# Batch 0's squares: summed over the pairs of heads by GpSimd ahead of TensorE

## The chip, the cores and the metric

The kernel runs on one core of one Trainium2 chip. The metric is the device time of one execution in microseconds (us), lower is better. The kernel before takes 975.91 us, the median of three runs (975.13 to 976.47).

## The reference, cut to what matters

Attention with keys and values pooled over 8 tokens (8 batches, 8 heads, 576 tokens, head size 64) feeds a gated MLP on 4608 tokens of width 512 with 1536 hidden units. Between the two stands an RMS norm: each token's 512 values x are divided by the root of the mean of their squares.

```python
rms = np.sqrt(np.mean(x * x, axis=-1, keepdims=True) + 1e-06)
xn = x / rms * rms_g
g = xn @ w_gate
val = xn @ w_val
return (silu * val @ w_out).astype(np.float32)
```

The 512 values of a token are 4 pairs of heads of 128 values. Attention's result lies with these 128 values on the partitions and the tokens along the free axis, one tile per pair of heads. The sum of squares of a token therefore runs over 128 partitions and over four tiles.

## The kernel before, in words

Work is done in 8 batches of attention and in blocks of 512 tokens of the MLP, interleaved. The order of everything is one long string, ORDER, of short step names; an underscore marks steps of the opening stage (attention of batches 0 and 1, the unpacking of the weights, the first MLP block). Each engine (TensorE, VectorE, ScalarE, GpSimd) and the queue of SyncE, which issues all DMAs, carries out its own instructions strictly in the order of the string. Waits between engines are put in by the framework: an instruction waits for what it reads, and a tile that takes over a place in memory waits until everything that the program does with the previous tile of that place is done. A step's name ends in hexadecimal-like digits: its numbers; a digit behind ":" is the PSUM bank, one behind "/" the buffer that it takes.

The steps that matter here, each with its line or helper:

- `_A` (s_av, L560) multiplies probabilities and values into PSUM tile psx, half the tokens at a time; for example `_A030` and `_A031` for pair 3 of batch 0.
- `_Z` (s_xsq, L590, ScalarE) squares psx into columns 2S to 3S of the tile own(p) of its pair p. There are eight: four pairs, two halves.
- `_P` (s_tokens, L652, TensorE) multiplies 128-token pieces of those squares by a column of ones, which sums over the partitions: five pieces, so five products per pair. They are float32 products, and the profile has two rows for each. Pair p writes column t * 4 + p of the PSUM tile psr.
- `_p` (s_total, L657, VectorE) adds the four pairs' columns, `_r0` (s_root, L664, ScalarE) takes the root, `_s0` (s_unroot, L667, VectorE) the reciprocal, `_B00` (s_spread, L676, TensorE) spreads it over the partitions, `_n` (L1029, ScalarE) copies it out of PSUM, and `_u0` (first_gate, L1033, VectorE) is the first to use it: it multiplies the first gate's psg, which `_m000` to `_m003` (first_mm, L1049, TensorE) produced, by it.
- `_l` loads a packed piece of the weights (L307, SyncE), `_a` reads it on ScalarE (L318), `_b`, `_c`, `_d` go on with it on VectorE (L322, L326, L330), `_h` rounds it on ScalarE (L344), `_w` or `_W` takes the rest (L292, VectorE or GpSimd). `_l6` to `_h6` is piece 6.
- `_N` (s_norm, L468) normalises probabilities of batch 1 on GpSimd; `_T` (L536) transposes them on TensorE.
- `_J` (s_join) adds two pairs' squares on GpSimd. Before the change only batches 1 and up use it; it goes through cut, which splits the 576 columns into two adds of 288.

Two places in memory are shared. own(0), the tile with pair 0's squares, lies in the slot w1_10. Piece 6 is the whole of the first weight matrix's block f = 3, and its raw words go to the slot NF - 1 - f % 2 = 10, the same one:

```python
s["own"] = space1(NF - 2 - 2 * p, [P, 3 * S + SP + P], F32, f"own{p}")
raw[f] = space1((2, 3)[f] if f < 2 else NF - 1 - f % 2, [P, 2 * NC * P, 2], U32, f"wx{f}")
```

In ORDER `_P00` stands before `_l6`, and `_P01 _P02 _P03` behind it. `_a6` is ScalarE's next step behind `_Z31`; then come `_h` of piece d (13), `_x31`, `_r0`. PSUM bank 2 is psr's, and the next to take it is `_T101:2`, ahead of `_B00` on TensorE.

Of the kernel before, what the change touches and what calls it, by code (L numbers as in the profile page):

```python
# [27 lines left out]
TOK = P  # L28
OFFS = (0, 128, 256, 384, 448)
# [33 lines left out]
_m011 _m001 _m013 _D100 _a9/0 _m003 _n _W4 _m100:5 Wt0/1 _l8 _Y031 _c6 _d6 _W7 _v11 _a8 _T102 _u0 _G0 _h6 _A100:1/1
_S11:27 _b9 _C102 _c9 _d9 _M110 _h9 _m102 _E110 _b8 _m110 _m112 _M111 _F0 _w9 _m101 _W6 _c8 _i0/1 _L0 Wf00 _d8 _lb/0
_R110 _m111 _K12/1 _A101:4 _ab/1 _X101 _bb _B01:6 _h8 _H01 _cb _m103 _u1 wf01 _db Wf02 _E111 _w8 _G1 _m113 _F1 wh03/0
Wl03 _la _X100 _hb _Wb _lf/0 Wf03 ws03 _e2:0 _o0:7564 _aa _g2:3 _i1/1 _ba _ca _L1 wh02/1 _o1 wl02 _af/0 _u2 _G2 _R111
_bf _cf _F2 _N110 _Q10 wd0 _i2/1 _T110:2/1 _D110 _df _hf _Wf _da _j2 _ha _g3:1 _lc _q12 _e3:0 wh01/0 _V11/0 _u3 _G3
_wa ws02 _o2 _N111 _F3 _ac _bc _cc _dc _k13 _i3/0 _lh/0 _ah/1 _hc _g4 _T112:1 _bh _D112 _j3 _T111:3 _le _D111 _e4:0
_ch _u4 _dh _hh wl01 ws01 Wt1/0 wh04/0 _ae Wl04 _Wc Wf10 _S12:32 _lg _Wh Wf11 Wf12 wf13 _be _M120 _M121 ws04 _G4 _F4
wh11/1 wl11 _ce _de _A110:1 _v20/1 _V20/1 _Y110 ws11 _o3 _A111:1 wh13/0 wd1 _i4/0 Wt2/1 _E120 _g5:0 wh14/1 _R120 Wl14  # L70
ws14 Wf20 _li Wl13 _L4 ws13 _ag _o4 _bg _e6 _he _We Wf21 _u5 _cg _E121 _R121 _dg wf22 _N121 wh12/1 Wl12 _e5:2 ws12 _G5
_Y111 _T121:1/1 Wf23 _F5 _i5/0 wh23/0 _v12 _j5 _N120 _D121 Wl23 wh21/1 Wl21 _q13 _K13/1 _T122 _ai _bi _ll/0 _hg ws23
ws21 _Wg _g6 _u6 _V12/0 _D122 _lk _k20 _v13 _o5 _G6 wh22/1 _F6 _i6/1 _ci _S13:10 _M130 _T120:3 _di wh24/0 Wl24 _D120
_j6 wl22 _M131 _g7 _u7 _hi ws22 _e7 _ak _o6 _K20/1 _bk _ck _G7 _F7 ws24 _E130 _dk _A121:3 _al/1 _bl _cl _ln/1 _an/0
_bn _cn _dl _i7/1 _R130 _dn _E131 _R131 _N131 _A120:2 _Y120 _hn _Wn _j7 _Y121 _g8:1 _u8 _V13/0 _G8 _wi _N130 wd4 _e8:0
_F8 _hl _wl _lj/0 _aj/0 _bj _cj _lm/1 _am/1 _bm _dj _T131:1/1 _o7 _D131 _hk _T130 _D130 _q20 sc20:21 wd2 _Q11/0 _cm
_T132 _D132 _dm _Wk _hj _A130:3 _Y130 Wt3/1 Wf30 _A131 _Y131 Wf31 lv21/0 mx201/1 sb201 _hm _Wj _wm _J11 mx200/1 lk21
pv21/0 _e9 sb200 wh33/0 Wl33 ex201 _lo/0 _i8/1 _L8 _g9:1 _u9 _ga:0 wh31/1 _o8 Wl31 ex200 _Q12/1 Wf32 Wf33 _J12 _Q13/0
ws33 _G9 _F9 ws31 _J13 _i9/0 wh34/0 pk21/1 Wl34 ws34 sm201/0 _ao/1 _bo _co _do _ho wh32/0 _L9 _P10:2 _ea _o9 _Wo _ua
sm200/0 nm200 _Ga _lp/0 _r1 Wl32 zd2 ws32 _Fa _ia/0 lq21 _ap/1 _gb:3 Nm201 tr20/1 _bp _La _s1 _B11:1 wd5 _cp _dp _hp  # L80
_ub _Gb _H11 wt4/0 _B10 _H10 _wp _eb:2 dm20 _Fb _oa sc21:10 wf40 wh41/0 Wl41 _t0 ws41 _t1 _ib/1 _jb wf41 wh43/1 _ob
lk22 Wl43 _t2 ws43 _t3 dp20/0 me10:2 Zt00/1 mg10:3 ev03/0 Wf42 Zt01 Zf00 Zf01 zh03/1 mx210/0 st03 sb210 Zl03 pk22/1
mx211/1 ev00/0 zs03 Zf02 Wf43 sb211 ex210 sm210/1 lq22 kt1 zh02/1 Zl02 ex211 sm211/1 st00 Nm210 zs02 wh42/0 Wl42 Nm211
av200:4/1 xc200 ws42 ev02/1 st02 me12:1 sc22:47 gt10 vl10 wh44/0 Wl44 hi10/0 lk23 ev01/1 mx221/1 ws44 st01 tr21/0
mx220/0 sb220 sb221 Lo10 mg11:6 Zf03 gt11 me11:0 dm21 vl11 zh04/0 zh01/1 mo10:4657 hi11/1 Zl04 zs04 mg12:0 Lo11 Zl01
Wt5/1 Wf50 mo11 wf51 wh53/0 Wf52 Wl53 zs01 pk23/0 gt12 vl12 av201:3 dp21/1 av210 ex220 xc210 av211:2 sm220/0 xd20 Wf53
xd21 lv23/0 wh54/1 Wl54 ws53 lq23 zd3 Nm220 pv23/0 ex221 sm221/1 Nm221 ws54 mg13:1 xc201 wh51/0 Wl51 tr22/0 xc211
hi12/1 sc23:03 mx231/0 mx230/1 sb230 ex230 sb231 lk30 pk30/1 wh52/1 Wl52 Lo12 dm22 ex231 lq30 me13:2 sm231/0 gt13
sm230/1 Nm230 vl13 Nm231 tr23/0 lv22/1 pv22/1 mo12 dp22/1 mg14:0 hi13/1 Lo13 ws51 me14 gt14 sc30:20 vl14 av221:1
mx301/1 xd22 sb301 dm23 sq20 sq21/1 Jn21 ws52 Wt6/0 av220:3 Wf60 Wf61 xc221 lk31 dp23/1 xc220 sq22/1 ex301 Jn22  # L90
mx300/0 pk31/0 mo13 hi14/1 lv30/1 sb300 Wf62 Lo14 wh61/0 Wl61 ws61 wh63/1 Wl63 ws63 wf63 mg15:0 gt15 sm301/0 nm301
lk32 ex300 me15 pv30/1 av231:2 xc231 wh64/0 sm300/0 Nm300 Wl64 av230:1 mo14 wh62/1 Wl62 lv31/1 ws64 xc230 vl15 tr30/0
hi15/0 Lo15 pk32/1 lq31 mg16:0 pv31/0 gt16 Zt10/1 ws62 Zf10 zh11/0 zl11 Zt11 Zf11 Zf12 me16:1 zh13/1 xd23 mo15 Zl13
dm30 vl16 sc31:20 mx310/0 zs11 sb310 zs13 mg17:1 hi16/1 Lo16 dp30/1 zh12/1 Zf13 zh14/0 mx311/0 mo16 sb311 zd4 gt17
Zl12 Zl14 Wt7/0 Wf70 zs14 Wf71 Wf72 wf73 sq23/1 Jn23 zs12 me17 ex310 av300:1/0 wh72/0 sm310/1 ex311 sm311/0 wh71/1
Wl71 xc300 lq32 zd1 vl17 hi17/1 Nm310 wl72 ws72 ws71 wh73/0 sh2/0 wh74/1 Nm311 tr31/1 sc32:02 mx320/0 sb320 av301:3
xd30 Lo17 dm31 ex320 xc301 Wl73 mx321/1 Wl74 Wt8/0 sb321 Wf80 mg18:1 ws73 gt18 Wf81 lk40 Wf82 ws74 wh81/0 mo17 Sl2
# [1112 lines left out]
```

## Time and profile before

| | before |
|---|---|
| median of 3 runs | 975.91 us |
| the profiled execution | 976.88 us |
| its span, first to last instruction | 975.1 us |
| TensorE matmuls busy | 947.5 us (97%) |
| VectorE busy | 704.2 us (72%) |
| ScalarE busy | 492.9 us (51%) |
| GpSimd busy | 490.4 us (50%) |
| mean granted TensorE clock | 0.982 of full speed |

The span is 1.8 us shorter than the execution's own time. An engine's busy time says how much it did, not what set the end; the chain of waits, followed back from the last instruction, says that. In the opening stage the share of each engine changes from microsecond to microsecond, so it is read from the order of time of single instructions. All times in the rows are microseconds from the start of the span.

### The profile page before, as it was taken

The numbers are of one execution on the slowest core, as the hardware profiler recorded it, in microseconds if no ns is written. First come the engines' busy times: TensorE is split into PE (matmuls) and PEld (weight loads), VectorE is DVE, ScalarE is ACT, GpSimd is POOL, SyncE is SP. The second block draws the span as 40 slices with busy tenths as digits, with TensorE's granted clock in tenths as the row PEclk, the third lists the DMA queues.
The fourth block names the chain that finished last, engine by engine and source line by source line (L and its number), as shares of the span: only waits on it lengthen the run. The fifth ranks groups of instructions, "written<-read, shape, count | busy, mean of one in ns | idle before, by whom it ended". The sixth has DMA issues, their size and how long they took to land.

```text
span 975.1 us, 14181 instructions
## 1 busy us (share of the span) xinstructions
PE 947.5 (97%) x4670; PEld 752.2 (77%) x4670; DVE 704.2 (72%) x1134; ACT 492.9 (51%) x929; POOL 490.4 (50%) x618
## 2 busy tenths in 40 slices
PE   7799999999999999999999999999999999999997
PEld 6577677777777877877877777877877778888885
DVE  6989898978787888778787877755565884433333
ACT  5876675645555647555455456242543642213332
POOL 3355637222322324433455788432296894445785
PEclk7789999999999999999999999999999999999999
DMA  9537774665766569878887776768686465767646
GB/s 300 183 137 273 225 247 157 215 204 178 240 204 204 171 182 267 251 231 274 253 248 255 202 253 195 243 184 263 217 257 212 155 219 173 229 189 232 205 141 204
DMA packets 142296, 211.41 MB, mean 217 GB/s; under 512 B 12240, under 2 KB 78288, under 8 KB 140944
## 3 DMA queue, kind: packets, MB, share of 16 engines
q1 hardware_dynamic: 142224, 210.52, 68.8%
q8 instruction: 37, 0.61, 0.3%
q14 instruction: 35, 0.29, 0.1%
HBM read 154.24 MB, written 56.23 MB: 216 GB/s over the span
## 4 chain that ended last, share of the span: by engine, by line
PE 76%; DMA 5%; DVE 5%; POOL 5%; ACT 3%; issue 2%; SPq 1%; DVEq 0%; ACTq 0%; POOLq 0%
PE pxy L895 30%; PE psg L1059 15%; PE pf L975 15%; PE po L1093 7%; PE psx L560 3%; PE pss L478 3%; POOL w L292 2%; DMA pt<-rows 1%; DMA ring<-vs 1%; POOL xp L292 1%; POOL hl L292 1%; DMA ring<-vB 1%; DVE wt L326 1%; PE psr L652 1%; DVE wt L330 1%
## 5 line engine op out<-in xcount | busy, mean ns | idle before, releaser
L895 PE MATMUL pxy<-xp,wp 128*128 128x512 f32 x1512 | 361.1, 391 | 1.5 <-ACT o L1104 0.7
L895 PEld LDWEIGHTS pxy<-xp,wp 128*128 128x128 f32 x1512 | 282.3, 188 | 65.3 <-issue 2.5
L975 PE MATMUL pf<-fp,ring 128*128 128x512 f32 x756 | 189.8, 393 | 3.1 <-DMA ring<-vB 1.6
L1059 PE MATMUL psg<-xh,w 128*128 128x512 f32 x544 | 171.2, 396 | 1.4 <-DVE prob L495 1.0
L975 PEld LDWEIGHTS pf<-fp,ring 128*128 128x128 f32 x756 | 139.6, 188 | 39.6 <-DMA ring<-vs 3.9
L1059 PEld LDWEIGHTS psg<-xh,w 128*128 128x128 f32 x544 | 101.2, 189 | 26.5 <-DVE prob L495 1.4
L1059 PE MATMUL psg<-xl,w 128*128 128x512 f32 x272 | 106.7, 392 | 0.0
L292 POOL TENSOR_TENSOR hl<-act,hh 128x256 fp32r<-128x256 f32 x58 | 49.8, 878 | 111.5 <-ACT hh L1075 102.6
L292 POOL TENSOR_TENSOR fp<-fs,fp 128x256 fp32r<-128x256 f32 x108 | 81.1, 778 | 41.7 <-ACT fp L948 37.9
L292 POOL TENSOR_TENSOR fp<-act,fp 128x256 fp32r<-128x256 f32 x72 | 55.1, 786 | 83.1 <-ACT fp L948 81.8
L1093 PE MATMUL po<-w,hh 128*128 128x512 f32 x288 | 72.9, 390 | 0.0
L292 POOL TENSOR_TENSOR w<-wt,w 128x256 fp32r<-128x256 f32 x50 | 48.7, 1000 | 45.7 <-ACT w L344 45.7
L1093 PEld LDWEIGHTS po<-w,hh 128*128 128x128 f32 x288 | 54.1, 188 | 11.6
L292 POOL TENSOR_TENSOR fp<-hb,fp 128x256 fp32r<-128x256 f32 x68 | 54.5, 828 | 13.9 <-ACT fp L948 13.9
L1059 PEld LDWEIGHTS psg<-xl,w 128*128 128x128 f32 x272 | 51.4, 189 | 11.1
L1154 ACT COPY hb<-pxy 128x512 f32<-128x512 f32 x36 | 21.0, 586 | 72.7 <-PE pxy L895 72.7
L1161 DVE TENSOR_TENSOR u<-u,pxy 128x512 f32<-128x512 f32 x36 | 24.7, 685 | 38.0 <-PE pxy L895 37.8
L948 ACT CAST fp<-act 128x512 fp32r<-128x512 f32 x36 | 22.2, 619 | 58.5 <-DVE act L1162 49.3
L948 ACT CAST fp<-fs 128x512 fp32r<-128x512 f32 x54 | 33.0, 618 | 34.3 <-POOL fs L292 16.7
L1155 DVE TENSOR_TENSOR u<-hb,pxy 128x512 f32<-128x512 f32 x36 | 24.6, 684 | 33.3 <-PE pxy L895 19.7
L292 POOL TENSOR_TENSOR fs<-act,hb 128x256 f32<-128x256 f32 x32 | 23.4, 752 | 50.0 <-DVE act L1162 28.0
L1158 DVE TENSOR_TENSOR hb<-u,pxy 128x512 f32<-128x512 f32 x36 | 24.7, 686 | 29.0 <-PE pxy L895 28.1
(193 smaller groups left out, 1636.0 us busy)
## 6 DMA issues: line engine op xcount, KB each, us to landing
wp<-sum SPq DMA_DIRECT2D x144, 256.0 KB
wp<-blocks SPq DMA_DIRECT2D x108, 256.0 KB
ring<-vs SPq DMA_DIRECT2D x72, 256.0 KB
ring<-vB SPq DMA_DIRECT2D x54, 256.0 KB
sum<-wt SPq DMA_DIRECT2D x48, 256.0 KB
blocks<-w SPq DMA_DIRECT2D x24, 512.0 KB
wx<-w SPq DMA_DIRECT2D x10, 1024.0 KB
v<-vN SPq DMA_DIRECT2D x32, 288.0 KB
```

The source lines that it names most:

```text
L292: getattr(eng, op)(*(x[..., o:o + step] for x in (out, a, b)))
L478: nc.tensor.matmul(s["ps", h][:, t * SP:(t + 1) * SP], s["q"][r, o:o + P], s["pk"][r, :], start=True, stop=True)
L560: nc.tensor.matmul(ps[r, :n], s["pv"][:, r], x, start=True, stop=True)
L895: nc.tensor.matmul(ps[:, :NB], w[:, a, c, :], x[:, b, c, :], start=j == 0 and not more, stop=j == len(todo) - 1, skip_group_check=more)
L948: nc.scalar.copy(y[:, 0], f_source(i, k, j))
L975: nc.tensor.matmul(ps[c], w[:, a, c * P:(c + 1) * P], x[:, b], start=j == 0 and n == 0 and not more, stop=j == HALF - 1 and n == 2, skip_g ...
L1059: nc.tensor.matmul(ps[:, :NB], w[:, c, cols], x[c], start=(j == 0), stop=(j == len(todo) - 1))
L1093: nc.tensor.matmul(po[i][t], x[i, f][:, t * P:(t + 1) * P], w, start=(f == 0 and k == 0), stop=(f == NF - 1 and k == 2))
L1154: cp=lambda i, f: S_.copy(later(i, f), st["XY", i, f, 0]),
L1155: u2=lambda i, f: V.tensor_add(u2(i, f), later(i, f), st["XY", i, f, 1]),
L1158: c2=lambda i, f: V.tensor_sub(later(i, f), u3(i, f), st["XY", i, f, 4]),
L1161: v1=lambda i, f: V.tensor_add(u2(i, f), u2(i, f), st["XY", i, f, 5]),
```

## The change: what it does

For batch 0 `_J` now adds pair p's squares onto pair 0's, in place, in own(0): three steps `_J02`, `_J01`, `_J03`, each two adds of 128x288 on GpSimd. `_P00` alone is left, behind `_J03`, and `_P01`, `_P02`, `_P03` and `_p` go. psr has five columns in place of twenty, and `_r0` reads it straight from PSUM. On GpSimd the joins stand ahead of `_N101`. The places of all other steps in ORDER are as before.

```diff
-_A000:5 _Z00 _h2 _W2 _D012 _T032:6 _D010 _v01 _A020:4 _k11 _d3 _h3 _l4 _P00:2 _V01 _C032 _w3 _R101 _A021:1 _v10 _x20
+_A000:5 _Z00 _h2 _W2 _D012 _T032:6 _D010 _v01 _A020:4 _k11 _d3 _h3 _l4 _V01 _C032 _w3 _R101 _A021:1 _v10 _x20 _y20
...
-_y20 _A010:3 _x00 _y00 _V10/0 _m000:7 _K11/1 _Y021 _x21 _y21 _Z21 _m010:6 _D031 _l7/0 _a7/1 _b7 _c7 _a4 _Z10 _ld/1 _l6
-_ad/0 _m002 _b4 _Z20 _bd _A011:5 _Y011 _Z11 _d7 _x11 _A030 _x30 _Z30 _cd _c4 _x10 _dd _A031:4 _Z31 _P01 _P02 _P03 _a6
-_hd _m012 _N101 _d4 _l9/0 _p _T100:1/1 _T101:2 _q11 _y30 _x31 _b6 _k12 _Wd _y11 _r0 _h7 _D101 _y31 _s0 _B00:5 _h4 _y10
+_A010:3 _x00 _y00 _V10/0 _m000:7 _K11/1 _Y021 _x21 _y21 _Z21 _m010:6 _D031 _l7/0 _a7/1 _b7 _c7 _a4 _Z10 _ld/1 _l6
+_ad/0 _m002 _b4 _Z20 _J02 _bd _A011:5 _Y011 _Z11 _J01 _d7 _x11 _A030 _x30 _Z30 _cd _c4 _x10 _dd _A031:4 _Z31 _J03
+_P00:2 _a6 _hd _m012 _N101 _d4 _l9/0 _T100:1/1 _T101:2 _q11 _y30 _x31 _b6 _k12 _Wd _y11 _r0 _h7 _D101 _y31 _s0 _B00:5
...
     def s_join(b, p, eng):
-        if p:
+        if b == 0:
+            x, y = (own(k)[:, 2 * S:3 * S] for k in (0, p))
+            cut(eng, "tensor_add", x, x, y, S // 2)
+        elif p:
             cut(eng, "tensor_add", acc[b], acc[b], st[b, p]["sq"], S // 2)
...
     def s_tokens(b, p):
-        if b or p == 0:
-            st["psr", b] = bank(0, f"psr{b}")
-        x = acc[b] if b else own(p)[:, 2 * S:3 * S]
+        st["psr", b] = bank(0, f"psr{b}")
+        x = acc[b] if b else own(0)[:, 2 * S:3 * S]
         for t, o in enumerate(OFFS):
-            nc.tensor.matmul(st["psr", b][:TOK, t * NP + p:t * NP + p + 1], x[:, o:o + TOK], one, start=True, stop=True)
-
-    def s_total():
-        t = st["total"] = const.tile([TOK, len(OFFS)], F32, name="total")
-        nc.vector.tensor_reduce(
-            t, st["psr", 0][:TOK, :len(OFFS) * NP].rearrange("p (t k) -> p t k", k=NP), AX.X, ALU.add)
+            nc.tensor.matmul(st["psr", b][:TOK, t:t + 1], x[:, o:o + TOK], one, start=True, stop=True)
...
-        x = st["psr", b][:TOK, :len(OFFS) * NP].rearrange("p (t k) -> p t k", k=NP)[:, :, 0] if b else st["total"]
-        nc.scalar.activation(r, x, AF.Sqrt, scale=1.0 / DM, bias=eps[:TOK])
+        nc.scalar.activation(r, st["psr", b][:TOK, :len(OFFS)], AF.Sqrt, scale=1.0 / DM, bias=eps[:TOK])
```

## Rows read from the trace of the kernel before

**Rows 1.** The page's chain that ended last, by engine, for the whole span; and the same chain in order of time from 44.65 us on (start, length, engine, line, how many instructions).

```profile
PE 76%; DMA 5%; DVE 5%; POOL 5%; ACT 3%; issue 2%; SPq 1%; DVEq 0%; ACTq 0%; POOLq 0%
...
44.65 0.71 PE psx L560 x4
45.36 6.01 PE psr L652 x30
51.37 1.49 PE psg L1049 x3
52.86 1.71 PE pst L536 x8
54.57 1.84 PE psb L676 x10
56.41 2.81 PE psg L1049 x12
```

**Rows 2.** Busy time by stretch: matmuls, weight loads, VectorE, ScalarE, GpSimd (instructions in brackets), then the granted TensorE clock (1.00 is 2.4 GHz, 0.50 is 1.2 GHz), DMA share and GB/s.

```profile
46.00:52.00 6.00, 6.00 (x28) 5.90 (x28) 3.43 (x6) 4.36 (x9) 1.67 (x2) 0.50 0.87 281
52.00:56.00 4.00, 4.00 (x20) 3.44 (x18) 4.00 (x8) 1.83 (x3) 0.00 (x0) 0.50 0.53 193
56.00:60.00 4.00, 4.00 (x20) 3.16 (x19) 2.00 (x4) 3.98 (x7) 3.79 (x4) 0.99 0.00 0
59.30:70.20 10.90, 10.90 (x67) 8.06 (x66) 10.85 (x16) 8.27 (x20) 9.79 (x11) 1.00 0.38 146
```

**Rows 3.** TensorE in order of time: single rows of the products that sum the squares, and the next step behind them (start, length, line, operation).

```profile
36.23 0.35 PE L652 MATMUL psr<-one,own 128*128 128x1 f32 x1
...
46.11 0.35 PE L652 MATMUL psr<-one,own 128*128 128x1 f32 x1
...
51.02 0.35 PE L652 MATMUL psr<-one,own 128*128 128x1 f32 x1
51.23 1.20 PE L1049 MATMUL psg<-xh,w 128*128 128x512 f32 x2
```

**Rows 4.** ScalarE in order of time: the squares of pair 2's and pair 3's last halves, `_a6`, the table load and `_r0`.

```profile
44.15 0.45 ACT L590 ACTIVATE own<-psx 128x288 f32<-128x288 f32 x1
...
46.22 0.49 ACT L590 ACTIVATE own<-psx 128x288 f32<-128x288 f32 x1
46.51 1.24 ACT L318 ACTIVATE wt<-wx 128x1024 f32<-128x1024 f32 x1
...
48.72 1.28 ACT L664 ACT_TABLE_LOAD   x1
51.62 0.30 ACT L664 ACTIVATE r<-total,eps 128x5 f32<-128x5 f32 x1 [1.62 <-DVE total L657]
```

**Rows 5.** The group of GpSimd's adds of two pairs' squares in the later batches: shortest, middle and longest duration in ns.

```profile
L292 POOL TENSOR_TENSOR acc<-acc,sq x14: 797/810/1337, 151.7 to 494.6; 128x288 f32<-128x288 f32 x14
```

**Rows 6.** VectorE in order of time while the squares are made, and its `_p`.

```profile
44.33 0.43 DVE L322 TENSOR_SCALAR wt<-wt 128x512 uint32<-128x512 uint32 x1 [0.17 <-ACT wt L318]
44.68 0.69 DVE L330 SCALAR_TENSOR_TENSOR wt<-wx,wt 128x512 uint32<-128x512 uint32 x1
45.28 0.68 DVE L326 SCALAR_TENSOR_TENSOR wt<-wx,wt 128x512 uint32<-128x512 uint32 x1
45.88 1.22 DVE L326 SCALAR_TENSOR_TENSOR wt<-wx,wt 128x1024 uint32<-128x1024 uint32 x1
47.02 0.68 DVE L330 SCALAR_TENSOR_TENSOR wt<-wx,wt 128x512 uint32<-128x512 uint32 x1
47.62 1.22 DVE L330 SCALAR_TENSOR_TENSOR wt<-wx,wt 128x1024 uint32<-128x1024 uint32 x1
51.41 0.18 DVE L657 TENSOR_REDUCE total<-psr 128x5 f32<-128x20 f32 x1 [2.57 <-PE psr L652]
```

**Rows 7.** GpSimd and VectorE beside each other, single instructions, first where VectorE's is of the same kind as in rows 6, and one of GpSimd with VectorE idle.

```profile
49.39 0.72 POOL L292 TENSOR_TENSOR w<-wt,w 128x256 fp32r<-128x256 f32 x1
...
60.00 0.92 POOL L292 TENSOR_TENSOR w<-wt,w 128x256 fp32r<-128x256 f32 x1
60.45 1.02 DVE L326 SCALAR_TENSOR_TENSOR wt<-wx,wt 128x512 uint32<-128x512 uint32 x1
60.89 1.17 POOL L292 TENSOR_TENSOR w<-wt,w 128x256 fp32r<-128x256 f32 x1
61.51 1.10 DVE L330 SCALAR_TENSOR_TENSOR wt<-wx,wt 128x512 uint32<-128x512 uint32 x1
62.02 1.19 POOL L292 TENSOR_TENSOR w<-wt,w 128x256 fp32r<-128x256 f32 x1
```

**Rows 8.** The DMA queue: the issues of `_ld` and `_l6` in order of time, the queue's wait by line, and what the DMAs moved in the stretches behind (columns as in rows 2).

```profile
35.97 0.33 SPq L307 DMA_DIRECT2D wx<-w  x1
36.66 0.33 SPq L307 DMA_DIRECT2D wx<-w  x1
...
SPq L307 <- PE psr L652: 0.3, 1, 0.3
...
36.00:38.00 2.00, 2.00 (x9) 1.24 (x11) 2.00 (x5) 1.94 (x6) 2.00 (x3) 0.50 0.49 141
38.00:40.00 2.00, 2.00 (x7) 1.17 (x4) 2.00 (x4) 0.35 (x2) 2.00 (x4) 0.50 1.08 432
```

**Rows 9.** VectorE's `_u0` in order of time, with the idle time ahead of it and what ended that.

```profile
59.31 0.69 DVE L1033 TENSOR_TENSOR act<-xraw,psg 128x512 f32<-128x512 f32 x1 [1.97 <-PE psg L1049]
```

More of the change, by code (lines that the diff above doesn't have):

```diff
@@ L63 @@
[L63 to L97, printed above, removed]
@@ L98 @@
-rm21:3 rt21 Wf83 wh84/1 Wl81 wl84 ws81 sm320/0 me18:2 vl18 dp31/1 rm20 rt20 hi18/1 Lo18 pk40/0 ws84 lv33/1 rc21 rs21
-wh82/0 Wl82 mg19:1 gt19 wh83/1 me19:2 av310:1 vl19 ex321 sm321/1 xc310 wl83 av311:3 lk33 xc311 mo18 hi19/0 pv33/0
+_A000:5 _Z00 _h2 _W2 _D012 _T032:6 _D010 _v01 _A020:4 _k11 _d3 _h3 _l4 _V01 _C032 _w3 _R101 _A021:1 _v10 _x20 _y20
+_A010:3 _x00 _y00 _V10/0 _m000:7 _K11/1 _Y021 _x21 _y21 _Z21 _m010:6 _D031 _l7/0 _a7/1 _b7 _c7 _a4 _Z10 _ld/1 _l6
+_ad/0 _m002 _b4 _Z20 _J02 _bd _A011:5 _Y011 _Z11 _J01 _d7 _x11 _A030 _x30 _Z30 _cd _c4 _x10 _dd _A031:4 _Z31 _J03
@@ new lines @@
+_P00:2 _a6 _hd _m012 _N101 _d4 _l9/0 _T100:1/1 _T101:2 _q11 _y30 _x31 _b6 _k12 _Wd _y11 _r0 _h7 _D101 _y31 _s0 _B00:5
+_h4 _y10 _m011 _m001 _m013 _D100 _a9/0 _m003 _n _W4 _m100:5 Wt0/1 _l8 _Y031 _c6 _d6 _W7 _v11 _a8 _T102 _u0 _G0 _h6
+_A100:1/1 _S11:27 _b9 _C102 _c9 _d9 _M110 _h9 _m102 _E110 _b8 _m110 _m112 _M111 _F0 _w9 _m101 _W6 _c8 _i0/1 _L0 Wf00
+_d8 _lb/0 _R110 _m111 _K12/1 _A101:4 _ab/1 _X101 _bb _B01:6 _h8 _H01 _cb _m103 _u1 wf01 _db Wf02 _E111 _w8 _G1 _m113
+_F1 wh03/0 Wl03 _la _X100 _hb _Wb _lf/0 Wf03 ws03 _e2:0 _o0:7564 _aa _g2:3 _i1/1 _ba _ca _L1 wh02/1 _o1 wl02 _af/0 _u2
@@ new lines @@
+_G2 _R111 _bf _cf _F2 _N110 _Q10 wd0 _i2/1 _T110:2/1 _D110 _df _hf _Wf _da _j2 _ha _g3:1 _lc _q12 _e3:0 wh01/0 _V11/0
+_u3 _G3 _wa ws02 _o2 _N111 _F3 _ac _bc _cc _dc _k13 _i3/0 _lh/0 _ah/1 _hc _g4 _T112:1 _bh _D112 _j3 _T111:3 _le _D111
+_e4:0 _ch _u4 _dh _hh wl01 ws01 Wt1/0 wh04/0 _ae Wl04 _Wc Wf10 _S12:32 _lg _Wh Wf11 Wf12 wf13 _be _M120 _M121 ws04 _G4
+_F4 wh11/1 wl11 _ce _de _A110:1 _v20/1 _V20/1 _Y110 ws11 _o3 _A111:1 wh13/0 wd1 _i4/0 Wt2/1 _E120 _g5:0 wh14/1 _R120
+Wl14 ws14 Wf20 _li Wl13 _L4 ws13 _ag _o4 _bg _e6 _he _We Wf21 _u5 _cg _E121 _R121 _dg wf22 _N121 wh12/1 Wl12 _e5:2
@@ new lines @@
+ws12 _G5 _Y111 _T121:1/1 Wf23 _F5 _i5/0 wh23/0 _v12 _j5 _N120 _D121 Wl23 wh21/1 Wl21 _q13 _K13/1 _T122 _ai _bi _ll/0
+_hg ws23 ws21 _Wg _g6 _u6 _V12/0 _D122 _lk _k20 _v13 _o5 _G6 wh22/1 _F6 _i6/1 _ci _S13:10 _M130 _T120:3 _di wh24/0
+Wl24 _D120 _j6 wl22 _M131 _g7 _u7 _hi ws22 _e7 _ak _o6 _K20/1 _bk _ck _G7 _F7 ws24 _E130 _dk _A121:3 _al/1 _bl _cl
+_ln/1 _an/0 _bn _cn _dl _i7/1 _R130 _dn _E131 _R131 _N131 _A120:2 _Y120 _hn _Wn _j7 _Y121 _g8:1 _u8 _V13/0 _G8 _wi
+_N130 wd4 _e8:0 _F8 _hl _wl _lj/0 _aj/0 _bj _cj _lm/1 _am/1 _bm _dj _T131:1/1 _o7 _D131 _hk _T130 _D130 _q20 sc20:21
@@ new lines @@
+wd2 _Q11/0 _cm _T132 _D132 _dm _Wk _hj _A130:3 _Y130 Wt3/1 Wf30 _A131 _Y131 Wf31 lv21/0 mx201/1 sb201 _hm _Wj _wm _J11
+mx200/1 lk21 pv21/0 _e9 sb200 wh33/0 Wl33 ex201 _lo/0 _i8/1 _L8 _g9:1 _u9 _ga:0 wh31/1 _o8 Wl31 ex200 _Q12/1 Wf32 Wf33
+_J12 _Q13/0 ws33 _G9 _F9 ws31 _J13 _i9/0 wh34/0 pk21/1 Wl34 ws34 sm201/0 _ao/1 _bo _co _do _ho wh32/0 _L9 _P10:2 _ea
+_o9 _Wo _ua sm200/0 nm200 _Ga _lp/0 _r1 Wl32 zd2 ws32 _Fa _ia/0 lq21 _ap/1 _gb:3 Nm201 tr20/1 _bp _La _s1 _B11:1 wd5
+_cp _dp _hp _ub _Gb _H11 wt4/0 _B10 _H10 _wp _eb:2 dm20 _Fb _oa sc21:10 wf40 wh41/0 Wl41 _t0 ws41 _t1 _ib/1 _jb wf41
@@ new lines @@
+wh43/1 _ob lk22 Wl43 _t2 ws43 _t3 dp20/0 me10:2 Zt00/1 mg10:3 ev03/0 Wf42 Zt01 Zf00 Zf01 zh03/1 mx210/0 st03 sb210
+Zl03 pk22/1 mx211/1 ev00/0 zs03 Zf02 Wf43 sb211 ex210 sm210/1 lq22 kt1 zh02/1 Zl02 ex211 sm211/1 st00 Nm210 zs02
+wh42/0 Wl42 Nm211 av200:4/1 xc200 ws42 ev02/1 st02 me12:1 sc22:47 gt10 vl10 wh44/0 Wl44 hi10/0 lk23 ev01/1 mx221/1
+ws44 st01 tr21/0 mx220/0 sb220 sb221 Lo10 mg11:6 Zf03 gt11 me11:0 dm21 vl11 zh04/0 zh01/1 mo10:4657 hi11/1 Zl04 zs04
+mg12:0 Lo11 Zl01 Wt5/1 Wf50 mo11 wf51 wh53/0 Wf52 Wl53 zs01 pk23/0 gt12 vl12 av201:3 dp21/1 av210 ex220 xc210 av211:2
@@ new lines @@
+sm220/0 xd20 Wf53 xd21 lv23/0 wh54/1 Wl54 ws53 lq23 zd3 Nm220 pv23/0 ex221 sm221/1 Nm221 ws54 mg13:1 xc201 wh51/0 Wl51
+tr22/0 xc211 hi12/1 sc23:03 mx231/0 mx230/1 sb230 ex230 sb231 lk30 pk30/1 wh52/1 Wl52 Lo12 dm22 ex231 lq30 me13:2
+sm231/0 gt13 sm230/1 Nm230 vl13 Nm231 tr23/0 lv22/1 pv22/1 mo12 dp22/1 mg14:0 hi13/1 Lo13 ws51 me14 gt14 sc30:20 vl14
+av221:1 mx301/1 xd22 sb301 dm23 sq20 sq21/1 Jn21 ws52 Wt6/0 av220:3 Wf60 Wf61 xc221 lk31 dp23/1 xc220 sq22/1 ex301
+Jn22 mx300/0 pk31/0 mo13 hi14/1 lv30/1 sb300 Wf62 Lo14 wh61/0 Wl61 ws61 wh63/1 Wl63 ws63 wf63 mg15:0 gt15 sm301/0
@@ new lines @@
+nm301 lk32 ex300 me15 pv30/1 av231:2 xc231 wh64/0 sm300/0 Nm300 Wl64 av230:1 mo14 wh62/1 Wl62 lv31/1 ws64 xc230 vl15
+tr30/0 hi15/0 Lo15 pk32/1 lq31 mg16:0 pv31/0 gt16 Zt10/1 ws62 Zf10 zh11/0 zl11 Zt11 Zf11 Zf12 me16:1 zh13/1 xd23 mo15
+Zl13 dm30 vl16 sc31:20 mx310/0 zs11 sb310 zs13 mg17:1 hi16/1 Lo16 dp30/1 zh12/1 Zf13 zh14/0 mx311/0 mo16 sb311 zd4
+gt17 Zl12 Zl14 Wt7/0 Wf70 zs14 Wf71 Wf72 wf73 sq23/1 Jn23 zs12 me17 ex310 av300:1/0 wh72/0 sm310/1 ex311 sm311/0
+wh71/1 Wl71 xc300 lq32 zd1 vl17 hi17/1 Nm310 wl72 ws72 ws71 wh73/0 sh2/0 wh74/1 Nm311 tr31/1 sc32:02 mx320/0 sb320
@@ L100 @@
+av301:3 xd30 Lo17 dm31 ex320 xc301 Wl73 mx321/1 Wl74 Wt8/0 sb321 Wf80 mg18:1 ws73 gt18 Wf81 lk40 Wf82 ws74 wh81/0 mo17
+Sl2 rm21:3 rt21 Wf83 wh84/1 Wl81 wl84 ws81 sm320/0 me18:2 vl18 dp31/1 rm20 rt20 hi18/1 Lo18 pk40/0 ws84 lv33/1 rc21
+rs21 wh82/0 Wl82 mg19:1 gt19 wh83/1 me19:2 av310:1 vl19 ex321 sm321/1 xc310 wl83 av311:3 lk33 xc311 mo18 hi19/0 pv33/0
 pk33/1 xd31 lv32/0 ws82 pv32/1 Zt20/0 Lo19 Zt21 Zf20 mg1a gt1a Nm321 Zf21 Zf22 zh22/0 Nm320 ws83 me1a:1 Zf23 zh24/1
@@ L1125, in first_steps @@
             A=s_av, Y=lambda b, p, u: s_xcopy(b, p, u, S_), X=lambda b, p, u: s_xcopy(b, p, u, V),
-            Z=s_xsq, Q=s_square, J=lambda b, p: s_join(b, p, G), P=s_tokens, p=s_total, r=s_root, s=s_unroot, B=s_spread, H=s_scale,
+            Z=s_xsq, Q=s_square, J=lambda b, p: s_join(b, p, G), P=s_tokens, r=s_root, s=s_unroot, B=s_spread, H=s_scale,
             x=first_hi, y=first_lo, n=first_norm, m=first_mm, u=first_gate,
```

## The prediction

> **What bounds the kernel now.** I read the chain of waits first. Over the whole span it lies on TensorE for 76%, so a delay of TensorE's early work is paid at the end unless a later wait swallows it. In order of time the chain then shows where the change falls: from 45.36 us it runs through the fifteen products of `_P01` to `_P03`, 30 rows and 6.01 us, then `_m012`, the transposes, `_B00`, twelve rows of `_m011` to `_m003`, and hands over to VectorE's `_u0` at 59.31 [rows 1, 9]. So this stage is TensorE's from 45 to 59, and the twenty products are on the path. The view by stretch adds two things: from 46 to 56 TensorE's clock is granted at 0.50, that is 1.2 GHz, though the engine is busy throughout; and from 59.30 to 70.20 VectorE is busy 10.85 of 10.90 us [rows 2], so what `_u0` loses is not won back there. Third, the single instructions of ScalarE, VectorE and GpSimd between 44 and 51, for the new adds stand among them; last the DMA queue, since the change moves the last use of own(0).
>
> **What goes.** `_P01` to `_P03`: 51.23 - 45.36 = 5.9 us of TensorE on the path [rows 1, 3]. `_P00` (ten rows, early) is moved behind them, so its old place is free; but TensorE takes the last psx at 44.65 only when ScalarE's square of 44.15 to 44.60 has freed its bank, and ScalarE takes `_Z31` at 46.22 in its own order [rows 1, 4]: earlier products change neither, and I count nothing. `_p` is 0.18 us of VectorE, with 2.57 us of idle time before it [rows 6]; but VectorE stands idle again for 1.97 us ahead of `_u0`, waiting for TensorE [rows 9], so that freed time only lengthens the later wait: nothing.
>
> **What comes: six adds on GpSimd.** Free of disturbance one takes 0.80 to 0.81 us, at worst 1.34 [rows 5]. `_J02` can start when pair 2's squares end, 44.60, say 44.65. Lower bound: 6 x 0.81 = 4.9, end at 49.5 (`_Z31` ends at 46.71 and isn't what is late). But VectorE runs instructions with two operands from SBUF back to back from 44.68 to 48.84 [rows 6]. What happens then has its own group: GpSimd's subtraction alone takes 0.72; beside the same VectorE instructions it takes 1.17 and 1.19, and VectorE's 0.68 becomes 1.02 and 1.10 [rows 7]; and the ends alternate: GpSimd 60.92, VectorE 61.47, GpSimd 62.06, VectorE 62.61, GpSimd 63.21. Each waits for the whole of the other. That gives 0.55 for a 512-wide VectorE step and 0.59 for a 256-wide GpSimd step; a 288-wide add is 0.81 - 0.73 = 0.08 longer, 0.67; a 1024-wide VectorE step 1.22 - 0.68 = 0.54 longer, 1.09. From 44.76, where the tensor_scalar ends [rows 6]: six adds, 4.02, with three 512-wide and two 1024-wide steps between them, 3 x 0.55 + 2 x 1.09 = 3.83, end at 52.6. Upper bound: all six at 1.34 is 8.0, the same 52.7. I take 52.6, because every instruction in the way is of the same kind [rows 7].
>
> The Trainium skill has this as a rule ("SBUF — State Buffer", "Who interferes with whom"): a VectorE instruction with two SBUF inputs and a GpSimd instruction that reads SBUF exclude each other for the whole instruction, and one with at most one SBUF input doesn't contend. By that rule the sum is the 52.6, without it 49.5; it speaks against putting these adds beside weight unpacking.
>
> **The five products left.** They start at about 52.65. At the slow clock a row takes (51.02 - 46.11) / 23 = 0.213 us [rows 3]; ten rows 2.1, so `_m012` starts at 54.8 in place of 51.23: 3.55 us late. At the fast clock they would take at most (46.11 - 45.36) / 6 = 0.125 a row, 1.2; after 7 us of idle TensorE I take the slow one.
>
> **What is moved past the DMA queue.** Piece 6 of the weights is loaded into the slot of own(0), and may start only when own(0) is done with. Before, that is `_P00`: its last row ends at 36.58, the queue issues `_l6` at 36.66, and the queue's one wait for that line, 0.3 us, names it [rows 3, 8]. After the change own(0) is read by `_P00` until about 52.65 + 9 x 0.213 + 0.35 = 54.9. `_l6` stands in its old place, so the queue stops there and issues it at 55.0; `_l9`, `_q11`, `_k12`, `_l8`, `_v11` stand behind it. Landing: before, the DMAs moved 141 x 2 = 0.28 MB from 36 to 38 and then 432 GB/s; 1.05 MB were through at 39.8, 3.8 us from the first issue at 35.97, and both loads (1.57 MB) at 41.0, 4.3 from the second [rows 8]. I take 4.0 (3.8 to 5.0): landed at 59.0.
>
> That load's reader is `_a6`, which ScalarE took at 46.51 without waiting [rows 4]. It stands ahead of `_h` of piece d, `_x31`, the table load and `_r0`. From `_a6`'s start to the end of that table load is 50.00 - 46.51 = 3.49 us [rows 4]. So `_a6` at 59.05, table loaded at 62.55, `_r0` done at 62.85; before, 51.92. psr's bank is `_T101`'s next, and now `_r0` itself frees it: `_T101` (half of the transposes' 1.71, 0.85) to 63.75 and `_B00`, 1.84, to 65.6 [rows 1]. Then the twelve rows: 2.81 at the fast clock, up to 4 x 1.49 = 5.96 at the rate of `_m012` [rows 1]. Before, the clock was back at 56, as `_B00` ended [rows 2]; now TensorE rests some 5 us ahead of `_T101`, so it may come later. I take 3.5: end at 69.1, `_u0` at 69.2, 9.9 us late. VectorE's own work ahead of `_u0` isn't later: behind `_s0` (63.1) stand about 0.4 of `_y10` and three 1024-wide steps of 1.2 each [rows 6], to 67.
>
> What follows `_u0` is late by the same 9.9, engines and DMAs alike, since the DMAs are triggered by it. The sum against the profiled execution is 976.9 + 9.9 = 986.8; the runs' median is 1.0 below that execution, so **985.8**.
>
> **The rivals.**
> - *The load is not held* (own(0)'s slot is free in time some other way, or ScalarE doesn't need it there). For it: the load had 46.51 - 41.0 = 5.5 us to spare before `_a6` [rows 4, 8]. Against: the queue's 0.3 us wait [rows 8], and a hold of 18 us is more than that. Then only the late products count, +3.5: 979.4.
> - *The adds aren't held by VectorE*, the load is: all 3.1 us earlier, +6.8: 982.7. Against it: the alternating ends [rows 7].
> - *Neither*: the adds end at 49.5, the products at 51.7 in place of 51.23, +0.45: 976.4, no change that can be told.
> - *Faster: the clock stays up.* It fell to 1.2 GHz at 46, just as the narrow products ran [rows 2, 3]. If these brought the fall, and resting doesn't, the five products take 1.3 and `_m012` starts at 50.85 (-0.4), and `_m012`, transposes and `_B00`, 1.49 + 1.71 + 1.84 = 5.0 [rows 1], run in half: -2.9 in all, 973.0. It decides only where the adds end before 50 and the load isn't held; against it stand both waits [rows 7, 8].
>
> **How the numbers follow.** Forecast 0.72, load not held 0.12, adds not held 0.08, neither 0.04, faster 0.04. A measurement of this kernel tells 0.2%, 2.0 us, from no change; so faster 0.04, same 0.04, slower 0.92. The forecast's own range is 983 to 989: landing up to 1.0 later, the twelve rows 0.7 shorter or 2.5 longer, and up to 2 swallowed by later waits. With the cases of 979.4 and 982.7 it becomes 979 to 989, which leaves out the last two.
>
> **What would show it.** In the profile after: `_a6` (L318) on ScalarE with some 12 us of idle time before it, put down to a DMA; the queue's wait at L307 for psr (L652) of many us in place of 0.3; six adds on GpSimd between 44.7 and 52.6, most of them over 1.1 us; `_r0` near 63 and `_u0` near 69; ten rows of psr in place of forty. If `_l6` is issued near 37, the load's step is wrong; if the adds end before 50, the step on VectorE is; if `_u0` is 10 us late but the end isn't, a later wait swallowed it. If the time is below 978, I have misread what is late in this stage.

## The result and the profile after

The changed kernel takes 986.67 us, the median of 4 runs (985.26 to 987.92), beside 976.19 us before (975.13 to 977.37). The ratio is 1.0101 with a 95% interval of 1.0079 to 1.0124: 10.5 us slower by the medians, 7.7 to 12.1 by the interval. The prediction was 985.8.

| | before | after |
|---|---|---|
| the profiled execution, its span | 976.88, 975.1 us | 987.92, 986.1 us |
| GpSimd busy | 490.4 us | 499.3 us |
| matmul instructions | 4670 | 4640 |
| mean granted clock | 0.982 | 0.974 |

The page of the profile after, busy time and the chain that ended last, by engine:

```profile
PE 947.5 (96%) x4640; PEld 751.1 (76%) x4640; DVE 707.0 (72%) x1133; ACT 492.8 (50%) x929; POOL 499.3 (51%) x624
...
PE 75%; POOL 6%; DMA 4%; DVE 4%; ACT 3%; issue 3%; SPq 1%; DVEq 0%; ACTq 0%; POOLq 0%
```

TensorE's instructions went down by 30 and its busy time stayed at 947.5 us, while the span grew by 11.0. So the loss is not more work on TensorE; it is waiting. The six adds brought GpSimd 7.95 us of work. The chain in order of time shows where the time went; the rows of before are in [rows 1].

```profile
45.69 1.40 POOL own L292 x2
...
51.12 1.78 POOL own L292
...
52.94 2.31 PE psr L654 x10
...
55.32 4.76 DMA wx<-w
...
60.10 1.12 ACT wt L318
...
62.09 1.28 ACT L659
...
63.39 0.28 ACT r L659
...
63.80 1.04 PE pst L536 x4
64.84 2.03 PE psb L671 x10
66.87 3.51 PE psg L1044 x12
...
70.47 0.69 DVE act L1028
```

Before, this stretch was TensorE's alone. Now it passes from GpSimd's adds to the five products, from their end to a DMA, from the DMA to ScalarE, and returns to TensorE at 63.80. The waits of the DMA queue and of ScalarE by line, from 20 to 80 us, name the two ends of that detour (us in all, times, longest):

```profile
SPq L307 <- PE psr L654: 17.9, 1, 17.9
...
ACT wt L318 <- DMA wx<-w: 12.4, 1, 12.4
```

The queue's wait for psr was 0.3 us [rows 8]; ScalarE had read that piece without waiting [rows 4].

The multiplication `_u0` starts at 70.47 in place of 59.31, 11.16 later, and the span is 11.0 longer, so what was lost by then was still lost at the end. About 1.1 us of it is not the change: in this execution `_Z31`, which starts ahead of everything that the change could delay, starts at 47.30 in place of 46.22. In a second profile of the changed kernel (e9 below) it starts at 46.29, `_u0` at 69.80, and the span is 985.7. Below, stage times are therefore read from `_Z31`'s start: `_u0` follows it by 13.09 us before, by 23.17 and 23.51 in the two profiles after. The rows are `_Z31` after, then `_Z31` and `_u0` in e9; those of before are in [rows 4] and [rows 9].

```profile
47.30 0.42 ACT L590 ACTIVATE own<-psx 128x288 f32<-128x288 f32 x1
...
46.29 0.44 ACT L590 ACTIVATE own<-psx 128x288 f32<-128x288 f32 x1
...
69.80 0.69 DVE L1028 TENSOR_TENSOR act<-xraw,psg 128x512 f32<-128x512 f32 x1 [2.55 <-PE psg L1044]
```

GpSimd and VectorE after the change, single instructions in order of time:

```profile
45.69 1.34 POOL L292 TENSOR_TENSOR own<-own,own 128x288 f32<-128x288 f32 x1 [4.84 <-ACT own L590]
45.69 0.68 DVE L330 SCALAR_TENSOR_TENSOR wt<-wx,wt 128x512 uint32<-128x512 uint32 x1
46.30 1.28 DVE L326 SCALAR_TENSOR_TENSOR wt<-wx,wt 128x512 uint32<-128x512 uint32 x1
46.99 1.24 POOL L292 TENSOR_TENSOR own<-own,own 128x288 f32<-128x288 f32 x1
47.50 1.81 DVE L326 SCALAR_TENSOR_TENSOR wt<-wx,wt 128x1024 uint32<-128x1024 uint32 x1
48.19 1.77 POOL L292 TENSOR_TENSOR own<-own,own 128x288 f32<-128x288 f32 x1
...
52.16 0.50 DVE L1018 SCALAR_TENSOR_TENSOR xl<-psx,gmean,xh 128x288 fp32r<-128x288 f32 x1
52.85 0.79 POOL L292 TENSOR_TENSOR own<-own,own 128x288 f32<-128x288 f32 x1
```

The same add takes 1.24 behind a 512-wide VectorE instruction, 1.77 behind a 1024-wide one, and 0.79 as the last of the six, when VectorE is idle. VectorE's 0.68 becomes 1.28 in turn. Its instruction at 52.16, whose other operand comes from PSUM, isn't held: it takes 0.50 while the fifth add runs, and took 0.51 with GpSimd idle before. The six adds take 7.95 us, from 45.69 to 53.64.

### The profile page after: what moved, and what is told of

The parts are those of the page before. It is cut to its first block, busy times and chain, and to the rows that moved or that the text cites. A ratio compares the mean times of both kernels' runs of the same rounds, so it can differ in the third digit from the quotient of the medians.

```text
span 986.1 us, 14129 instructions
## 1 busy us (share of the span) xinstructions
PE 947.5 (96%) x4640; PEld 751.1 (76%) x4640; DVE 707.0 (72%) x1133; ACT 492.8 (50%) x929; POOL 499.3 (51%) x624
## 4 chain that ended last, share of the span: by engine, by line
PE 75%; POOL 6%; DMA 4%; DVE 4%; ACT 3%; issue 3%; SPq 1%; DVEq 0%; ACTq 0%; POOLq 0%
PE pxy L890 31%; PE psg L1054 15%; PE pf L970 14%; PE po L1088 8%; PE psx L560 3%; PE pss L478 3%; DMA wx<-w 2%; POOL fp L292 2%; POOL xp L292 2%; POOL w L292 1%; ACT wt L318 1%; DMA ring<-vB 1%; DMA pt<-rows 1%; DVE wt L326 1%; DVE wt L330 1%
## 5 line engine op out<-in xcount | busy, mean ns | idle before, releaser
L292 POOL TENSOR_TENSOR fp<-act,fp 128x256 fp32r<-128x256 f32 x72 | 54.8, 783 | 82.8 <-ACT fp L943 81.6
```

## The experiments

All times below are medians; each is compared with runs of the kernel before on the same chip. The theory of the prediction has two prices: the load of piece 6, which waits for own(0), and the adds, which wait for VectorE.

**e1: the load set free.** Pair 0's squares and the sum go to a slot that is empty until batch 1.

```diff
+    def squares(p):
+        if p:
+            return own(p)[:, 2 * S:3 * S]
+        if "squares" not in st[0, 0]:
+            st[0, 0]["squares"] = sb1.tile([P, S], F32, tag="acc", name="squares0")
+        return st[0, 0]["squares"]
...
-            x, y = (own(k)[:, 2 * S:3 * S] for k in (0, p))
+            x, y = squares(0), squares(p)
```

> The changed kernel, with pair 0's squares and their sum in the slot acc instead of own(0), so that the load of weight piece 6 waits no longer for the five products; the adds stay on GpSimd. Theory (the load's hold costs about 6.5 us and the adds beside VectorE about 3.5): ScalarE takes the piece near 46.5 without waiting, the adds still end near 52.5, the products end near 54.8, the gate's first multiplication comes 3 to 4 us later than before: 3.5 us slower than the kernel before, about 979.5. Rival (the late sum alone is the whole loss): 9 to 11 us slower, as the change.

Measured: 980.34 us beside 976.68, ratio 1.0030 (1.0011 to 1.0049). The adds, `_a6` and `_u0` in its profile:

```profile
44.81 8.41 POOL L292 TENSOR_TENSOR squares<-squares,own 128x288 f32<-128x288 f32 x6 [4.85 <-ACT own L597]
...
46.66 1.20 ACT L318 ACTIVATE wt<-wx 128x1024 f32<-128x1024 f32 x1
...
63.24 0.69 DVE L1035 TENSOR_TENSOR act<-xraw,psg 128x512 f32<-128x512 f32 x1 [4.08 <-PE psg L1051]
```

ScalarE takes the piece at 46.66 without waiting. The adds take 8.41 us, 0.46 more than in the changed kernel, and 3.7 us of the loss are left by the medians. The rival, that the late sum is the whole loss, falls.

**e2: the hold alone.** No adds; the kernel before, with pair 0's five products put behind pair 3's.

```diff
-... _l4 _P00:2 _V01 ... _Z31 _P01 _P02 _P03 _a6
+... _l4 _V01 ... _Z31 _P01:2 _P02 _P03 _P00 _a6
```

> The kernel before, with all twenty products and no adds, but the five of pair 0 put behind those of pair 3, so that own(0) is held until then. Theory: the load of piece 6 is issued near 53.5 in place of 36.7, its reader on ScalarE starts near 58.3 (4.8 us from issue, as in the changed kernel), the gate's first multiplication near 68.7: 9 us slower, about 985. Rival (the hold is harmless, the adds on GpSimd are the loss): only the five products' 2.1 us on the path, about 978.

Measured: 985.94 us beside 976.68, ratio 1.0087 (1.0051 to 1.0123). From its chain and its single instructions:

```profile
54.42 4.73 DMA wx<-w
...
59.16 1.12 ACT L318 ACTIVATE wt<-wx 128x1024 f32<-128x1024 f32 x1 [12.00 <-DMA wx<-w]
...
68.86 0.69 DVE L1033 TENSOR_TENSOR act<-xraw,psg 128x512 f32<-128x512 f32 x1 [1.55 <-PE psg L1049]
```

This kernel has not one added instruction. It has the same twenty products, five of them in another place, and is 9.3 us slower. The late end of own(0)'s use, and nothing of GpSimd, brings the detour over the DMA.

**e3: the adds on VectorE, the load still held.** GpSimd and VectorE no longer meet.

```diff
-J=lambda b, p: s_join(b, p, G)
+J=lambda b, p: s_join(b, p, G if b else V)
```

> The changed kernel with the three joins on VectorE, one add of 576 each, in the same places of the order; the load of piece 6 is still held. Theory: VectorE's adds take about 0.7 us each and never wait for GpSimd, the last ends near 50 (before: 52.5 on GpSimd), the load is issued near 52.3, its reader starts near 57.1, the gate's first multiplication near 67.5: 7 to 8 us slower, about 983.5. Rival (GpSimd's adds are the main cost): at most 1 us slower, about 977.

Measured: 985.35 us beside 976.68, ratio 1.0080 (1.0051 to 1.0109).

```profile
50.34 0.75 DVE L292 TENSOR_TENSOR own<-own,own 128x576 f32<-128x576 f32 x1
...
58.32 1.12 ACT L318 ACTIVATE wt<-wx 128x1024 f32<-128x1024 f32 x1 [10.52 <-DMA wx<-w]
...
69.43 0.69 DVE L1028 TENSOR_TENSOR act<-xraw,psg 128x512 f32<-128x512 f32 x1 [2.92 <-PE psg L1044]
```

Its `_Z31` starts at 47.37, 1.15 later than before, so the adds' end of 51.09 and `_a6` at 58.32 are the forecast's 50 and 57.1. `_u0` comes 0.8 later than that forecast by the same reading. That lies in the twelve rows: they take 4.23 us (65.09 to 69.32) in place of 3.51, since the clock is granted at 0.50 up to 68 us here as in the changed kernel, where they start 1.8 later. The time is 8.7 us above the kernel before by the medians, where 7 to 8 were expected; the interval, 5.0 to 10.6, holds both. Fast adds alone save little while the load is held: `_u0` follows `_Z31` by 22.06 in place of 23.17 and 23.51.

**e4: both mended.** e1 with e3's line.

> Both: the joins on VectorE and pair 0's squares in the slot acc. Theory: neither cost is left; the last add ends near 50, the five products near 52.1 in place of 51.2: 0 to 1.5 us slower, about 977. Rival (something else of the change costs, such as the removed sum on VectorE or the bank that the root frees): more than 3 us slower.

Measured: 977.69 us beside 976.68, ratio 1.0001 (0.9982 to 1.0021).

```profile
49.42 0.75 DVE L292 TENSOR_TENSOR squares<-squares,own 128x576 f32<-128x576 f32 x1
...
50.22 2.30 PE L661 MATMUL psr<-one,squares 128*128 128x1 f32 x10 [4.18 <-DVE squares L292]
...
60.91 0.69 DVE L1035 TENSOR_TENSOR act<-xraw,psg 128x512 f32<-128x512 f32 x1 [3.74 <-PE psg L1051]
```

With both prices gone the loss is gone. It is also not a gain: fifteen products fewer, and no difference from the kernel before that can be told. TensorE stands idle for 4.18 us until the last add is done, and the five products behind it end at 52.52, 1.15 later than the fifteen had ended (51.37).

**e5: half as many adds.** e1 with each join as one add of 576 columns. If each add waits for one whole VectorE instruction, fewer adds wait less; if GpSimd is slower by the column, nothing changes.

```diff
-            cut(eng, "tensor_add", x, x, y, S // 2)
+            cut(eng, "tensor_add", x, x, y, S)
```

> The kernel of e1 (pair 0's squares in the slot acc, the load free, the joins on GpSimd), with each join as one add of 576 columns in place of two of 288: the same columns, half the instructions. Theory (each GpSimd add waits for the whole of one VectorE instruction, and then runs at its own rate): three adds of about 1.45 us with two 512-wide VectorE instructions of 0.55 between them end 5.5 us after they begin, near 50.2, in place of 8.4 after; the gate's first multiplication comes 2 to 3 us earlier than in e1, about 978 in all. Rival (GpSimd beside VectorE is slower by the column): the adds take 8 us as in e1, and the time is e1's, 980.

The adds and `_u0` in its profile:

```profile
44.67 1.95 POOL L292 TENSOR_TENSOR squares<-squares,own 128x576 f32<-128x576 f32 x1 [4.87 <-ACT own L597]
...
46.70 1.73 POOL L292 TENSOR_TENSOR squares<-squares,own 128x576 f32<-128x576 f32 x1
...
48.51 2.26 POOL L292 TENSOR_TENSOR squares<-squares,own 128x576 f32<-128x576 f32 x1
...
60.99 0.69 DVE L1035 TENSOR_TENSOR act<-xraw,psg 128x512 f32<-128x512 f32 x1 [2.07 <-PE psg L1051]
```

The same columns take 6.1 us (44.67 to 50.77) in place of 8.41, and `_u0` comes 2.25 us earlier than in e1 (2.13 behind `_Z31`): for the adds the theory held, its rival fell. VectorE is late for it: the same five weight steps end at 53.05, in e1 at 51.37. In the whole time the gain did not show: 980.26 us beside 975.70, ratio 1.0044 (1.0027 to 1.0061). So e1, e5 and the changed kernel were run again on one chip.

**e7, e8, e9: the three on one chip.** The kernels of e1, e5 and the changed one.

> e1 once more, beside e5 and the changed kernel on one chip, since e1 and e5 were timed on two. Theory (what the gate's first multiplication gains in this stage is there at the end, and the two chips and the scatter of single executions hid it): 2 us above e5, 6.5 us below the changed kernel. Rival (the stage's gain of e5 over e1 is swallowed by a later wait): the same as e5 within 1 us.

> e5 once more, beside e1 on the same chip. Theory: 2 us below e1, 1.5 to 2.5 us above the kernel before. Rival: the same as e1 within 1 us.

> The changed kernel once more, on the same chip. Both theories: 10 us above the kernel before; its distance to e1, 6.5 us by the theory of the load's hold, is what is read.

Measured, beside 976.20 us before: 979.87 for e1's (1.0033, 1.0018 to 1.0048), 978.98 for e5's (1.0024, 1.0009 to 1.0039), 986.62 for the changed kernel (1.0098, 1.0072 to 1.0125). By these medians the changed kernel's loss of 10.4 us (7.0 to 12.2 by its interval) splits into 986.62 - 979.87 = 6.75 us for the load's hold and 3.67 us (1.8 to 4.7) for the late sum. The two do not simply add: with fast adds the hold costs 985.35 - 977.69 = 7.66 (e3, e4), and of the 3.67 e4 keeps 1.0 by the medians, which can't be told from nothing.

e5's time is 0.9 us below e1's, the intervals overlap, and the first pair of runs had it the other way. The second pair of profiles shows why the gain is uncertain. The adds take 8.41 and 6.09 us again, and `_B00` starts 11.33 and 11.30 us behind `_Z31` with six adds (e1, e7), 9.86 and 9.88 with three (e5, e8): 1.4 us gained, both times. But `_u0` follows `_Z31` by 16.87 and 15.75 with six, 14.74 and 15.17 with three, so the gain there is 2.13 in the first pair and 0.58 in the second. Between the two steps lies the return of the clock: in the stretch from 58 to 60 us it is granted at 0.50 in e1 and 0.82 in e7, and from `_B00`'s start to `_u0`'s pass 5.5 us in e1 and 4.4 in e7. The rows are `_u0` in e7 and e8, then that stretch in e1 and in e7.

```profile
62.55 0.69 DVE L1035 TENSOR_TENSOR act<-xraw,psg 128x512 f32<-128x512 f32 x1 [2.99 <-ACT wt L318]
...
61.02 0.69 DVE L1035 TENSOR_TENSOR act<-xraw,psg 128x512 f32<-128x512 f32 x1 [2.47 <-PE psg L1051]
...
58.00:60.00 2.00, 2.00 (x11) 2.00 (x11) 1.16 (x1) 2.00 (x4) 0.45 (x1) 0.50 0.00 0
...
58.00:60.00 2.00, 2.00 (x15) 1.92 (x14) 1.52 (x2) 1.65 (x3) 0.05 (x1) 0.82 0.00 0
```

Whether three adds beat six in the whole time is left open.

**e6: a version meant to beat both.** The kernel before with pair 0's products early as they were; VectorE adds pairs 2 and 3 onto pair 1's squares, the second add ahead of two of its weight steps; ten products, and piece d's rounding behind the root.

```diff
-... _Z11 _d7 ... _cd _c4 _x10 _dd _A031:4 _Z31 _P01 _P02 _P03 _a6 _hd ... _Wd _y11 _r0 _h7
+... _Z11 _J02 _d7 ... _cd _x10 _A031:4 _Z31 _J03 _c4 _dd _P01 _a6 ... _y11 _r0 _hd _Wd _h7
...
+        if b == 0:
+            x, y = (own(k)[:, 2 * S:3 * S] for k in (1, p))
+            cut(eng, "tensor_add", x, x, y)
```

> A version meant to beat both: the kernel before with pair 0's five products early as they were (so the load of piece 6 is free), pairs 2 and 3 added onto pair 1's squares by VectorE, the second add placed right behind the last squares and ahead of two 1024-wide and 512-wide weight steps, five products for that sum, and the rounding of piece d moved behind the root on ScalarE. Theory: the last add ends near 47.7, the products near 49.9 in place of 51.2, the gate's first multiplication 1 to 1.5 us earlier than before: 1.2 us faster, too little to be sure of against the kernel before, but 11 us faster than the changed one. Rival (VectorE's own chain, 1.5 us longer ahead of the gate, or the clock coming back later, takes it back): 0 to 2 us slower than before.

Measured: 976.43 us beside 975.70, ratio 0.9994 (0.9974 to 1.0013).

```profile
47.05 0.75 DVE L292 TENSOR_TENSOR own<-own,own 128x576 f32<-128x576 f32 x1
...
47.85 2.09 PE L655 MATMUL psr<-one,own 128*128 128x1 f32 x10 [2.20 <-DVE own L292]
...
58.05 0.69 DVE L1036 TENSOR_TENSOR act<-xraw,psg 128x512 f32<-128x512 f32 x1 [1.07 <-PE psg L1052]
```

The stage went as forecast: `_Z31` starts at 46.41, `_u0` 11.64 us later in place of 13.09, a gain of 1.45. The whole time can't be told from the kernel before; single executions of that kernel on this chip run from 973.92 to 980.72, so a gain of this size stays unproven. It beats the changed kernel clearly, the kernel before not measurably.

## Why the prediction was right

The forecast case came true. It had 9.9 us, of which its first rival gives 3.5 to the late sum alone; the runs give 10.4, of which 3.67 without the hold. The steps, with the profile after put back by the 1.08 us that its `_Z31` came late:

| step | predicted | after, less 1.08 |
|---|---|---|
| last add ends | 52.6 | 52.56 |
| five products start | 52.65 | 51.86 |
| `_m012` starts | 54.8 | 54.02 |
| load of piece 6 issued | 55.0 | 54.24 |
| `_a6` starts | 59.05 | 59.02 |
| `_r0` done | 62.85 | 62.59 |
| twelve rows done | 69.1 | 69.30 |
| `_u0` starts | 69.2 | 69.39 |

- **The adds.** Alternating whole instructions, 0.67 and 0.55 or 1.09 us a step, gave the end of the last add to 0.05 us. The two-operand VectorE instructions and the adds hold each other up, as the rule cited of the Trainium skill has it ("SBUF — State Buffer", "Who interferes with whom"). Of the rule's second half the prediction left out a condition: that page of the Trainium skill says that a VectorE instruction with at most one SBUF input doesn't contend "outside the 2-port perf modes". In e1 a VectorE instruction with one SBUF input does hold the last add, which ends 0.65 us behind it (52.57, 53.22) as the others do; whether it ran in such a mode no run here shows.

```profile
51.72 0.85 DVE L322 TENSOR_SCALAR wt<-wt 128x1024 uint32<-128x1024 uint32 x1
...
51.98 1.24 POOL L292 TENSOR_TENSOR squares<-squares,own 128x288 f32<-128x288 f32 x1
```

- **The products' start** was put 0.8 us too late. I let TensorE wait for the whole of `_J03`; its first products read only columns that the first of the two adds writes.

```profile
52.94 2.29 PE L654 MATMUL psr<-one,own 128*128 128x1 f32 x10 [6.57 <-POOL own L292]
55.10 1.20 PE L1044 MATMUL psg<-xh,w 128*128 128x512 f32 x2
```

  They start as the fifth add ends (51.12 + 1.77 = 52.89), not the sixth (53.64).
- **The load's landing** was put 0.8 us too short: 4.76 us from issue to landing, 4.73 in e2, where I took 4.0 out of 3.8 to 5.0. In the trace after, the load's last packet ends at 59.70, 4.38 us from the issue, and the reader's release follows 0.38 later; so half of the miss is the time of the bytes, half the release, which I had left out. The reading of rows 8 was too fast as well: I carried the 432 GB/s of 38 to 40 us on, but from 40 to 41 the DMAs moved 369 and from 41 to 42 only 49, and the last packet of the two loads ended at 42.36, not 41.0. A page of the Trainium skill ("DMA: Bandwidth & Descriptors", "Anatomy of one DMA — SWDGE (gpsimd) path") gives about 2.0 us fixed plus the bytes at 436 GB/s, for DMAs that GpSimd issues; 1.05 MB make 4.4 by it, an estimate nearer to the 4.76 than mine. That these two errors, in the products' start and in the landing, cancelled is luck.
- **ScalarE's queue** behind the late load ran nearly as in rows 4, 3.28 us from `_a6`'s start to the loaded table in place of 3.49. `_T101` waited for `_r0`, which frees psr's bank now: TensorE stood idle 6.22 us ahead of it. In e2, where `_p` frees the bank, `_T101` is through before, and `_B00` starts 0.28 us after `_r0`'s end (62.75, 63.03) in place of 0.97 (63.66, 64.63). So some 0.7 us of the loss is the bank's, by this estimate.

```profile
63.80 1.04 PE L536 MATMUL pst<-ident,prob 128*72 128x128 f32 x4 [6.22 <-ACT r L659]
```

- **The clock.** The views by stretch (columns as in [rows 2]):

```profile
56.00:66.60 10.60, 4.38 (x20) 3.47 (x20) 4.29 (x8) 5.75 (x9) 1.52 (x3) 0.50 0.87 331
66.60:70.40 3.80, 3.80 (x15) 3.10 (x15) 1.69 (x1) 3.78 (x6) 3.80 (x5) 0.79 0.00 0
```

  It stood at 1.2 GHz until `_B00` was through and came back within the twelve rows, so these took 3.51 on the chain in place of 2.81. The 3.5 of the prediction was picked between 2.81 and 5.96, and that it was hit is partly luck: in e9, the same kernel, they took 3.87. The rival in which it stays at 2.4 GHz because the narrow products are gone is refuted: it was granted at 0.50 from 48 to 52 us, when TensorE rested and no product had begun.

```profile
48.00:52.00 4.00, 0.00 (x0) 0.00 (x0) 4.00 (x3) 0.00 (x0) 4.00 (x4) 0.50 0.00 0
```

- **The end.** Nothing later swallowed the delay: 11.16 us at `_u0`, 11.0 at the end of the profiled span.
- **The cost at nothing** for `_p` held: VectorE stands idle 2.17 us ahead of `_u0`, after 1.97 before.
- **The second rival's price** was too low. Fast adds with the load held (e3) lose 8.7 us by the medians, and `_u0` comes 8.97 later behind `_Z31`, where the prediction had 6.8 (the interval of e3 holds that too). The adds ended 2.6 us earlier, not 3.1, and the slow twelve rows took back a part.

## What to carry to other kernels

Before moving the last use of a tile, look up who takes its place in memory: here a load, on an in-order queue, whose reader stood ahead of the critical step, and moving five products behind it made 6.75 us of loss, by the medians, while fifteen others were saved. Adds handed to GpSimd beside VectorE instructions with two operands in SBUF wait for one whole instruction each, so count instructions, not columns. And fifteen products saved are worth only what the sum that replaces them can be early by: e4, without either loss, came out even.

## What was not expected

Three adds of 576 columns took 6.1 us where six of 288 took 8.41 (e5, e1): beside a busy VectorE larger instructions on GpSimd finish sooner in sum. VectorE's five weight steps end 1.7 us later there. The stage's begin differs from one execution to the next: `_Z31` starts between 45.85 and 47.37 us in the eleven profiles. In the profiles of e1 and e4 the span departs from the shift of `_u0` by 2.0 and -2.5 us. Single executions of the kernel before run from 972.72 to 980.65 us on one chip and from 973.92 to 980.72 on another, so a change of a few us can't be read from a single execution.
